# Products of probabilities with v issued for two key tiles in every second unit of attention

## The chip, the cores and the metric

The kernel runs on one core of one Trainium2 chip. The metric is device microseconds for one execution, and less is better. The core's engines each work through their own instructions in order and wait for each other by semaphores: TensorE (PE in the profile, its weight loads apart as PEld), VectorE (DVE), ScalarE (ACT), GpSimd (POOL), and SyncE (SP), which here issues most of the DMA.

## What is computed

Three layers one after the other, of which the change touches the first. Attention runs over 2 batches, 8 heads, 768 positions and a head dimension of 64; a query sees only the keys whose six projection signs equal its own. The layers behind it, a mixture of eight experts and a SoLU network, are not touched.

```python
q_bits = (np.einsum('bhsd,dk->bhsk', q, proj) > 0).astype(np.int64)
k_bits = (np.einsum('bhsd,dk->bhsk', k, proj) > 0).astype(np.int64)
mask = q_bucket[:, :, :, None] == k_bucket[:, :, None, :]
scores = scale * np.matmul(q, k.transpose(0, 1, 3, 2))
scores = np.where(mask, scores, -1000000000.0)
scores = scores - np.max(scores, axis=-1, keepdims=True)
attn = np.exp(scores)
attn = attn / (np.sum(attn, axis=-1, keepdims=True) + 1e-09)
return np.matmul(attn, v).astype(np.float32)
```

## The kernel before

**Units.** Attention is cut into 96 units. A unit is one tile of 128 queries of one head against all 768 keys. Six units (two heads by three query tiles) make a block j, and there are sixteen blocks; two blocks make one pair of heads n. The main loop (in the function that builds the kernel, behind the line that gets `emit_pv`) runs over the units i from 0 to 95 and records each unit's work; the order on every engine is the order in which the code records it, since the schedule is written by hand.

**What a unit i records**, in this order:

- `emit_s(i)` (L537): four matmuls of the scores s into one of two PSUM tiles, namely two halves of the keys, each first with the values and then with the sign bits. Between them and behind them stand the six transposes of the probabilities of unit i-2 (`steps_t`, L576), three into PSUM tile t0 and three into t1, with one buffer each. ScalarE copies each of the two to SBUF as pt (L578).
- in every sixth unit `fin_a` (L622): VectorE copies the finished sums v of a block from PSUM to xt. v has one PSUM buffer.
- `emit_max(i)` (L547, L549, L551): VectorE takes the largest score of each row, and two short steps behind it.
- `emit_exp(i)` (L562): ScalarE makes the probabilities p from s and the maximum.
- `emit_pv(jj, c)` (L595): the probabilities of block jj times v for the key tile c. For i from 8 to 91 jj and c are the quotient and the rest of i-8 by 6, so one of the six key tiles is done in each unit. It is two float32 matmuls, one for each head, which fill two halves of the columns; the trace shows each of them as two records. A block's tile c = 0 begins the sums in v, and c = 5 ends them.
- the background steps set for this unit. Those that matter here: `fin_b` in units 6j+14 (matmuls L638 from xt, on VectorE L627 to L658); `bits`, matmuls (L499 for q, L501 and L503 for k) and VectorE steps (L509) that make the sign bits of the next pair of heads, in units 5, 6, 9, 10 and 11 of each twelve; and, in three stretches, the routing of the next layer (`route_a` and others, L688 to L745).

So the order on PE within a unit is: scores and transposes, then the two v matmuls, then background matmuls. On ACT it is: the two copies of the transposes, then the exponential. On DVE: xt if there is one, the maximum, then background steps.

**What waits for what.** The scores of unit i need the PSUM tile that the exponential of unit i-2 has read. The transposes in unit i need the probabilities of unit i-2, and they need t0 and t1 to have been copied out by ACT, whose copies of the unit before stand behind the exponential of unit i-2. The v matmuls of c = 0 need the v tile to have been copied to xt; the L638 matmuls need xt itself.

**After the loop** the last blocks are done in other groupings (units 92 and 93 do three key tiles of block 14 each), and then come the experts.

Of the kernel before, what the change touches and what calls it, by code (L numbers as in the profile page):

```python
# [21 lines left out]
def kernel(  # L22
# [191 lines left out]
    def setup_first():  # L214


        fi = const.tile([128, 3], F32, name="fi")
        io = const.tile([128, 1], I32, name="io")
        nc.gpsimd.iota(io, pattern=[[0, 1]], base=0, channel_multiplier=1)
        nc.gpsimd.memset(pw, 0.0)  # L220
        d = nc.vector
        d.tensor_scalar(out=io, in0=io, scalar1=31, scalar2=None, op0=ALU.bitwise_and)
        d.tensor_copy(out=fi[:, 0:1], in_=io)
        d.tensor_scalar(out=fi[:, 1:2], in0=fi[:, 0:1], scalar1=float(NBIT), scalar2=-TINY, op0=ALU.is_ge, op1=ALU.mult)
        d.tensor_scalar(out=fi[:, 2:3], in0=fi[:, 0:1], scalar1=float(2 * NBIT), scalar2=TINY, op0=ALU.is_ge,
                        op1=ALU.mult)
        d.tensor_copy(out=thr[:, 1:2], in_=fi[:, 1:2])
        d.scalar_tensor_tensor(out=thr[:, 0:1], in0=fi[:, 1:2], scalar=TINY, in1=fi[:, 2:3], op0=ALU.add, op1=ALU.add)

    def setup_late():  # L230
        ie = const.tile([128, E], I32, name="ie")
        it = const.tile([128, B, NS], I32, name="it")
        g = nc.gpsimd
        g.memset(rb, 0.0)
        for h in range(2):
            r = slice(64 * h, 64 * h + 64)
            for wi, w in enumerate((w_gate, w_ogate)):
                c0 = 128 + 16 * h + 8 * wi
                nc.sync.dma_start(out=rb[r, :, c0:c0 + 8],
                                  in_=w.rearrange("(c h p) e -> h p c e", h=2, p=64)[h])  # L240
        nc.sync.dma_start(out=g1, in_=g_ln.rearrange("(f p) -> p f", p=128))
        g.iota(ie, pattern=[[1, E]], base=0, channel_multiplier=0)
        g.iota(it, pattern=[[S, B], [1, NS]], base=0, channel_multiplier=NS)
        make_upper_triangular(nc, upper, val=1.0, diag=False)
        g.memset(ones16, 1.0)
        g.memset(nhalf, -0.5)
        g.tensor_copy(out=iota8, in_=ie)
        g.tensor_copy(out=me[:, :, 1], in_=it.rearrange("p b s -> p (b s)"))
        g.tensor_scalar(out=iota_s, in0=iota8, scalar1=1.0 / 16.0, scalar2=1.0, op0=ALU.mult, op1=ALU.mult)
        g.tensor_scalar(out=ord0, in0=iota8, scalar1=-1.0, scalar2=1.0, op0=ALU.mult, op1=ALU.mult)  # L250
        for e in range(2):
            g.memset(ord0[:, e:e + 1], float(16 * NT * (2 - e)))
        for e in range(E):
            g.memset(caps[:, e:e + 1], float(CAPS[e]))
        for x in range(MW):
            g.memset(win_w[:, x:x + 1], float(WIN * x))
        g.tensor_scalar(out=row0, in0=iota8, scalar1=float(NT), scalar2=1.0, op0=ALU.mult, op1=ALU.mult)

        g.memset(hs, 0.0)
        g.tensor_scalar(out=hs[:, 0], in0=iota8, scalar1=float(NT // 128), scalar2=1.0, op0=ALU.mult, op1=ALU.mult)  # L260
# [617 lines left out]
    with tc.manual_schedule():  # L878
        with ExitStack() as es:
            A = attention(es)  # L880
            pj = A["pj"]
            cm, rb = A["cm"], A["rb"]
            setup_first()
            A["first"]()
            A["load"](1)
            setup_late()
            NU = A["NU"]
            bg = A["bg"]
            JL = 2 * NP - 2
            a_ = A.__getitem__  # L890
            pv, fa, tr = a_("emit_pv"), a_("fin_a"), a_("emit_t")
            for i in range(NU):
                a_("emit_s")(i, a_("steps_t")(i - 2) if 2 <= i else iter(()))
                if i in A["pre"]:
                    fa(A["pre"][i])
                a_("emit_max")(i)
                a_("emit_exp")(i)
                jj, c = divmod(i - 8, 6)
                if 0 <= jj < JL:
                    pv(jj, c)  # L900
                elif jj == JL and c < 2:
                    for x in range(3):
                        pv(JL, 3 * c + x)
                if i == NU - 3:
                    fa(JL, 0, 3, True)
                    a_("fin_r")(JL)
                if i == NU - 2:
                    a_("fin_mm")(JL)
                    a_("fin_l")(JL)
                    a_("fin_x")(JL)  # L910
                for f, a in bg.pop(i, []):
                    f(*a)
            assert not bg, bg.keys()

            J = JL + 1
            a_("route_a")(2)
            tr(NU - 2)
            for c in range(3):
                pv(J, c, 0, 2)
            a_("route_mm")(2)  # L920
            a_("route_b")(2)
            for c in range(3, NS):
                pv(J, c, 0, 2)
            fa(J, 0, 2)
            a_("fin_r")(J, 0, 2)
            a_("route_s")(2)
            tr(NU - 1)
            a_("fin_mm")(J, 0, 2)
            a_("fin_r")(J, 2, 3)
            for c in range(NS):  # L930
                pv(J, c, 2, 3)
            a_("fin_l")(J, 0, 2)
            a_("fin_x")(J, 0, 2, True)
            a_("route_a")(3)
            a_("route_mm")(3, tail=True)
            fa(J, 2, 3)
            a_("route_b")(3)
            a_("fin_mm")(J, 2, 3)
            a_("fin_l")(J, 2, 3)
            a_("route_a")(4)  # L940
            a_("route_mm")(4, (9, 10), True)
            a_("fin_x")(J, 2, 3, True, True)
            a_("route_b")(4)
            a_("route_s")(3)
            a_("totals")()
            for x in range(3):
                a_("route_d")(x, 2, 3, 4)
# [351 lines left out]
```

## Time and profile before

| | |
|---|---|
| median of 3 runs | 562.22 us (561.19 to 564.54) |
| time of the profiled execution | 566.43 us |
| its span, first to last instruction | 563.4 us |
| mean granted TensorE clock | 0.972 |
| PE busy | 515.2 us (91%), 3848 matmul records |
| DVE busy | 415.1 us (74%) |
| ACT busy | 339.6 us (60%) |
| POOL busy | 257.1 us (46%) |
| attention's units 8 to 91 | 28.23 to 242.91 us of the span |

The profile page gives busy times over the whole span, a strip of forty slices, the chain that ended last, and the costliest groups of instructions. The trace answers for single stretches: in a timeline each row has its start, its length, the engine, the line, the operation, output and inputs, and in brackets how long the engine sat idle before it and which instruction released it. Neighbouring records of one kind are merged into one row with their count.

### The profile page before, as it was taken

What the parts mean: (1) busy time and instruction counts of PE and PEld (TensorE: products, weight loads), DVE (VectorE), ACT (ScalarE), POOL (GpSimd) and SP (SyncE); (2) the same over time, 40 slices, a digit from 0 to 9 for tenths busy, and PEclk for the clock granted to TensorE, in tenths of its full rate; (3) what the DMA queues carried; (4) which work ended last, traced back from release to release, by engine and by line L of the source; (5) the groups of instructions that cost most, each with busy time, mean ns of one, the idle gap of its engine ahead of it and who ended that gap; (6) DMA issues with size and microseconds to landing.
All of it is one profiled execution on the core that took longest, in us unless ns stands there. A gap on an engine that the chain in (4) does not pass through costs nothing. (4 is left out here: it accounts for less than half of the span.)

```text
span 563.4 us, 10637 instructions
## 1 busy us (share of the span) xinstructions
PE 515.2 (91%) x3848; PEld 347.2 (62%) x3848; DVE 415.1 (74%) x929; ACT 339.6 (60%) x638; POOL 257.1 (46%) x321
## 2 busy tenths in 40 slices
PE   6799999999899999996499889599999999999994
PEld 5456565656555656664399789599997444444441
DVE  7877878788887898767339997799994776455440
ACT  6677787777667776863147866677572544344240
POOL 7968583838596674616036565222330111111112
PEclk9999999999999999999699999799999999999998
DMA  5576658554719263002498999999830242422542
GB/s 169 111 225 126 229 93 264 99 159 73 242 36 214 66 136 102 2 1 93 89 279 263 239 268 280 268 314 294 288 101 1 39 93 57 105 64 58 112 79 70
DMA packets 104487, 81.72 MB, mean 145 GB/s; under 512 B 79728, under 2 KB 86768, under 8 KB 104432
## 3 DMA queue, kind: packets, MB, share of 16 engines
q1 hardware_dynamic: 102128, 74.71, 51.5%
q0 software_dynamic: 2304, 6.31, 3.1%
q8 instruction: 31, 0.51, 0.4%
q14 instruction: 24, 0.20, 0.1%
HBM read 51.43 MB, written 9.97 MB: 109 GB/s over the span
## 5 line engine op out<-in xcount | busy, mean ns | idle before, releaser
L562 ACT ACTIVATE p<-s,mx 128x768 f32<-128x768 f32 x96 | 95.3, 992 | 55.4 <-DVE mx L551 46.0
L576 PE MATMUL t<-ident,p 128*128 128x128 f32 x576 | 126.1, 276 | 0.9 <-ACT pt L578 0.7
L547 DVE TENSOR_REDUCE mx<-s 128x1 f32<-128x768 f32 x96 | 91.7, 955 | 25.8 <-PE s L537 23.2
L578 ACT COPY pt<-t 128x384 f32<-128x384 f32 x192 | 84.7, 479 | 12.0 <-PE t L576 10.9
L576 PEld LDWEIGHTS t<-ident,p 128*128 128x128 f32 x576 | 78.4, 142 | 16.2 <-ACT pt L578 7.0
L1034 PE MATMUL a<-xw,wa 128*128 128x224 f16 (+5 forms) x256 | 65.4, 258 | 22.1 <-DVE yT L1075 12.1
L595 PE MATMUL v<-pt,v 128*64 128x384 f32 (+1 forms) x384 | 80.1, 503 | 2.9 <-DVE xt L622 2.5
L1045 POOL TENSOR_TENSOR hh<-hf,hh 128x448 f16<-128x448 f32 (+5 forms) x32 | 41.9, 1308 | 86.4 <-ACT hf L1044 86.3
L1246 PE MATMUL o<-wo,zT 128*128 128x512 f16 x288 | 64.0, 379 | 2.3 <-DMA zT<-z 2.3
L1035 PE MATMUL a<-xw,wa 128*128 128x224 f16 (+5 forms) x256 | 65.5, 258 | 0.0
L1036 PE MATMUL a<-xw,wa 128*128 128x224 f16 (+5 forms) x256 | 65.4, 258 | 0.0
L1065 PE MATMUL a<-hh,wb 128*128 128x224 f16 (+5 forms) x256 | 63.8, 252 | 0.5 <-DVE yT L1075 0.5
L1181 PE MATMUL h<-wi,yT 128*128 128x512 f16 x288 | 63.8, 379 | 0.1
L1066 PE MATMUL a<-hh,wb 128*128 128x224 f16 (+5 forms) x256 | 63.8, 252 | 0.0
L1067 PE MATMUL a<-hh,wb 128*128 128x224 f16 (+5 forms) x256 | 63.8, 252 | 0.0
L537 PE MATMUL s<-k,q 128*128 128x384 f16 x192 | 59.1, 332 | 4.0 <-ACT p L562 4.0
L537 PE MATMUL s<-b,cm 128*128 128x384 f16 x192 | 57.7, 328 | 1.1 <-DVE b L509 1.1
L1246 PEld LDWEIGHTS <-zT 128*128 128x128 f16 x288 | 27.9, 98 | 37.0 <-DMA zT<-z 3.7
L1181 PEld LDWEIGHTS <-yT 128*128 128x128 f16 x288 | 28.1, 98 | 34.1 <-DVE so L1207 0.6
L537 PEld LDWEIGHTS <-q 128*128 128x128 f16 x192 | 19.5, 102 | 39.6 <-issue 37.7
L1196 ACT ACTIVATE ex<-h,st,csc 128x1024 f32<-128x1024 f32 x12 | 14.5, 1204 | 44.3 <-DVE st L1219 36.0
L665 POOL TENSOR_SCALAR xh<-xf 128x384 f16<-128x384 f32 x15 | 7.7, 513 | 67.8 <-DVE xf L658 67.7
(241 smaller groups left out, 999.2 us busy)
## 6 DMA issues: line engine op xcount, KB each, us to landing
raw<-in_moe_w_dram SPq DMA_DIRECT2D x64, 512.0 KB, 5.3
raww<-in_moe_w_in_dram SPq DMA_DIRECT2D x8, 512.0 KB, 8.1
raww<-in_moe_w_out_dram SPq DMA_DIRECT2D x8, 512.0 KB
xs<-raw SPq DMA_DIRECT2D x8, 448.0 KB
v<-in_v_dram SPq DMA_DIRECT2D x8, 384.0 KB
q<-in_q_dram SPq DMA_DIRECT2D x7, 384.0 KB, 5.2
k<-in_k_dram SPq DMA_DIRECT2D x7, 384.0 KB, 4.5
cm<-q SPq DMA_DIRECT2D x14, 96.0 KB, 2.0
```

The costliest lines, as they stand in the source:

```text
L537: nc.tensor.matmul(t[:, c, 0:SB], d[x, h][:, s], flat(d[y, h])[:, c * SB:(c + 1) * SB], start=first, stop=not first)
L547: nc.vector.tensor_reduce(out=mx[:, 0:1], in_=t[:, :, 0:SB], op=ALU.max, axis=AX.XY)
L562: nc.scalar.activation(out=p, in_=s_t.pop(i)[:, :, 0:SB], func=AF.Exp, scale=mx[:, 1:2], bias=mx[:, 2:3], accum_out=sums[j][:, qt, h:h + 1])
L576: nc.tensor.transpose(t[:, g * 128:(g + 1) * 128], p[:, c, g * 128:(g + 1) * 128], ident)
L578: nc.scalar.copy(out=pt[j, h][:, 3 * c:3 * c + 3, qt * 128:(qt + 1) * 128], in_=t[:, 0:SB].rearrange("p (g c) -> p g c", g=3))
L595: nc.tensor.matmul(pv[j, q0][64 * h:64 * h + 64, 0:w], vt[:, h, c], pt[j, h][:, c, q0 * 128:q1 * 128], start=(c == 0), stop=(c == NS - 1), ...
L1034: nc.tensor.matmul(ps[:, i, 0:n], w[:, 0, kk, fs], xw[:, kk], start=(kk == 0), stop=False)
L1035: nc.tensor.matmul(ps[:, i, 0:n], w[:, 0, kk, fs], xw[:, KD + kk], start=False, stop=False)
L1036: nc.tensor.matmul(ps[:, i, 0:n], w[:, 1, kk, fs], xw[:, kk], start=False, stop=(kk == KD - 1))
L1065: nc.tensor.matmul(ps, w[:, 0, f, ds], hh[:, 0, f], start=(f == 0), stop=False)
L1181: nc.tensor.matmul(ps[:, c], yT[:, a, kk, ts], w_i[:, w, kk, c * 512:(c + 1) * 512], start=(kk == 0 and a == 0 and w == 0), stop=(kk == KD ...
L1246: nc.tensor.matmul(ps, zT[:, KF * a + f], w_o[:, w, f], start=(f == 0 and a == 0 and w == 0), stop=(f == KF - 1 and a == 1))
```

## The change

In units 8 to 91 the v matmuls are left out where the key tile c is even, and where c is odd those of c-1 and of c are recorded, in this order, at that place. As i-8 is even for even c, the even units record no v matmuls and the odd ones four. Unit 92 and those behind it are as before.

```diff
@@ -896,7 +896,8 @@
                 a_("emit_max")(i)
                 a_("emit_exp")(i)
                 jj, c = divmod(i - 8, 6)
-                if 0 <= jj < JL:
+                if 0 <= jj < JL and c % 2:
+                    pv(jj, c - 1)
                     pv(jj, c)
                 elif jj == JL and c < 2:
                     for x in range(3):
```

On PE, between units 24 and 25 (t are the transposes, v the products with the probabilities pt, s the scores of the next unit). Before:

```order
L576 MATMUL t_1107<-ident,p 128x128 x3
L595 MATMUL v<-pt_763,v 64x384
L595 MATMUL v<-pt_867,v 64x384
L537 LDWEIGHTS q_790
L537 MATMUL s<-k_853,q_790 128x384
L576 MATMUL t_1132<-ident,p 128x128
```

And now:

```order
L576 MATMUL t_1107<-ident,p 128x128 x3
L537 LDWEIGHTS q_787
L537 MATMUL s<-k_851,q_787 128x384
L576 MATMUL t_1130<-ident,p 128x128
L537 LDWEIGHTS q_787
```

The scores and transposes of unit 25 follow directly on the transposes recorded in unit 24.

On PE, at the end of unit 25. Before:

```order
L576 MATMUL t_1140<-ident,p 128x128 x3
L595 MATMUL v<-pt_763,v 64x384
L595 MATMUL v<-pt_867,v 64x384
L537 LDWEIGHTS q_790
L537 MATMUL s<-k_853,q_790 128x384
```

And now:

```order
L576 MATMUL t_1138<-ident,p 128x128 x3
L595 MATMUL v<-pt_763,v 64x384
L595 MATMUL v<-pt_865,v 64x384
L595 MATMUL v<-pt_763,v 64x384
L595 MATMUL v<-pt_865,v 64x384
L537 LDWEIGHTS q_787
```

Four v matmuls, for the key tiles 4 and 5 of the block, stand where two stood.

On PE, at the end of unit 26, where `fin_b` puts its matmuls m from xt. Before:

```order
L576 MATMUL t_1171<-ident,p 128x128 x3
L595 MATMUL v<-pt_964,v 64x384
L595 MATMUL v<-pt_1072,v 64x384
L638 MATMUL m<-rb,xt 128x160 x3
L537 LDWEIGHTS q_792
```

And now:

```order
L576 MATMUL t_1171<-ident,p 128x128 x3
L638 MATMUL m<-rb,xt 128x160 x3
L537 LDWEIGHTS q_789
L537 MATMUL s<-k_853,q_789 128x384
L576 MATMUL t_1205<-ident,p 128x128
```

The first matmuls that need VectorE's copy of the finished block are now those of L638. On the other engines the instructions stand in the order of before.

## Rows read from the trace of the kernel before

**Rows 1.** Busy time by engine in one cycle of twelve units; stretch, length, engines, PEclk, DMA share, GB/s
```profile
64.12:94.14 30.02, 29.90 (x208) 18.06 (x205) 24.13 (x56) 22.76 (x49) 19.41 (x22) 1.00 0.65 162
```
**Rows 2.** Waits in that cycle: engine, line, releaser; total, times, longest
```profile
ACT p L562 <- DVE mx L551: 7.2, 11, 0.9
```
**Rows 3.** PE timeline, first scores of units 6 and 7; unit 6 has no v matmuls
```profile
24.23 0.34 PE L537 MATMUL s<-k,q 128*128 128x384 f16 x1
...
25.55 0.33 PE L537 MATMUL s<-k,q 128*128 128x384 f16 x1
```
**Rows 4.** PE timeline, unit 93, which does three key tiles, and what follows in 94
```profile
247.32 0.33 PE L537 MATMUL s<-k,q 128*128 128x384 f16 x1
...
248.72 2.16 PE L595 MATMUL v<-pt,v 128*64 128x384 f32 x12
250.81 0.34 PE L537 MATMUL s<-k,q 128*128 128x384 f16 x1
...
252.13 0.98 PE L638 MATMUL m<-rb,xt 128*128 128x160 f32 x6
```
**Rows 5.** PE timeline, units 21 to 30 of that cycle
```profile
63.41 0.51 PE L501 MATMUL m<-k,pw 128*32 128x384 f16 x8
...
71.09 0.33 PE L576 MATMUL t<-ident,p 128*128 128x128 f32 x1
...
73.18 0.34 PE L537 MATMUL s<-k,q 128*128 128x384 f16 x1
...
75.38 1.08 PE L638 MATMUL m<-rb,xt 128*128 128x160 f32 x6
76.30 0.33 PE L537 MATMUL s<-k,q 128*128 128x384 f16 x1
76.46 0.27 PE L576 MATMUL t<-ident,p 128*128 128x128 f32 x1
...
78.50 0.34 PE L537 MATMUL s<-k,q 128*128 128x384 f16 x1
...
83.51 0.34 PE L537 MATMUL s<-k,q 128*128 128x384 f16 x1
```
**Rows 6.** PEld: the v matmuls' weight loads in that cycle; busy us, mean ns
```profile
L595 PEld LDWEIGHTS v<-pt,v 128*64 128x64 f32 x48 | 2.4, 134 | 2.2 <-issue 1.8 <-DVE xt L622 0.3
```
**Rows 7.** DVE timeline, units 22 to 27 of that cycle
```profile
66.81 1.25 DVE L509 TENSOR_SCALAR b<-m,thr 32x384 f16<-32x384 f32 x2
68.09 0.96 DVE L547 TENSOR_REDUCE mx<-s 128x1 f32<-128x768 f32 x1
...
69.52 0.62 DVE L509 TENSOR_SCALAR b<-m,thr 32x384 f16<-32x384 f32 x1
70.17 0.96 DVE L547 TENSOR_REDUCE mx<-s 128x1 f32<-128x768 f32 x1
...
72.23 0.96 DVE L547 TENSOR_REDUCE mx<-s 128x1 f32<-128x768 f32 x1 [0.66 <-PE s L537]
...
73.54 0.55 DVE L622 COPY xt<-v 128x384 f32<-128x384 f32 x1
...
75.75 0.22 DVE L627 TENSOR_SCALAR r<-sums 128x6 f32<-128x6 f32 x1
...
76.50 0.26 DVE L647 TENSOR_TENSOR lt<-m,r 128x96 f32<-128x96 f32 x1 [0.31 <-PE m L638]
...
77.56 0.95 DVE L547 TENSOR_REDUCE mx<-s 128x1 f32<-128x768 f32 x1
```
**Rows 8.** ACT timeline, exponential of unit 23
```profile
69.58 0.99 ACT L562 ACTIVATE p<-s,mx 128x768 f32<-128x768 f32 x1 [0.88 <-DVE mx L551]
```
**Rows 9.** PE timeline, unit 56, where routing work stands ahead of xt
```profile
151.27 0.87 PE L595 MATMUL v<-pt,v 128*64 128x384 f32 x4 [1.72 <-DVE xt L622]
```
**Rows 10.** Busy time by engine early in attention, and behind the wait of unit 56
```profile
15.00:28.00 13.00, 9.12 (x68) 6.08 (x65) 10.67 (x23) 8.65 (x18) 12.18 (x36) 1.00 0.59 120
...
152.50:155.90 3.40, 3.40 (x15) 2.64 (x13) 1.56 (x7) 1.56 (x3) 0.91 (x2) 0.50 0.03 10
```

## The prediction

> **What bounds the kernel now.** I first asked the trace for the busy time of one cycle of twelve units, the period after which the background work repeats. TensorE is busy 29.90 of 30.02 us at full clock (1.00, the 2.4 GHz level), VectorE 24.13 and ScalarE 22.76 [rows 1]. Read alone, that says that TensorE's work sets the end, and that any saving of it is a gain. So I asked next who waits for whom: nearly every exponential on ScalarE waits for VectorE's maximum (11 times, 7.2 us) [rows 2]. TensorE is full, but it runs just ahead of a chain that goes round every two units: last scores, maximum, exponential, then the transposes of these probabilities two units later. Third came the timelines of single units, to see how much slack that chain has, because the change alters the distance between a unit's scores and its transposes.
>
> **What is saved on TensorE.** A unit without v matmuls takes 25.55 - 24.23 = 1.32 us [rows 3], a plain one 78.50 - 76.30 = 2.20 [rows 5], so the two v matmuls of one key tile cost 0.89. Unit 93 does three key tiles and takes 250.81 - 247.32 = 3.49 [rows 4]: the second and third cost (3.49 - 2.20) / 2 = 0.645 each. Two key tiles together thus cost 1.54 where they cost 1.78, a saving of 0.245. The price is of the very form that the change makes, so I take it as it is.
>
> The Trainium skill speaks against so low a price: its page "TensorE: Matmul & The Clock Gate", section "Packing small matmuls — row/col tiling", says that a weight load overlaps running matmuls only if it goes to other rows of the array, and both v matmuls use all 128. By that rule a load, 0.134 us in the trace [rows 6], would stand ahead of each further tile and the saving would be about 0.11; the trace doesn't bear the rule out here, since the 0.645 of unit 93 already holds all loads.
>
> A second saving: the L638 matmuls now follow transposes, not v matmuls. Behind v they last 1.08 and the next scores come 0.92 after their start [rows 5], behind transposes they last 0.98 [rows 4]; I take 0.10 less, hence 0.82. A cycle has six merged pairs and two such places: 6 x 0.245 + 2 x 0.10 = 1.67 us. Units 8 to 91 are seven cycles: 11.7 us of TensorE's work.
>
> **What is added: waits.** The order of instructions on the other engines is unchanged, no DMA is moved, and POOL and SP get nothing new. What changes is that even units are short (1.32) and odd ones long (1.32 + 1.54 = 2.86). An odd unit's scores now come only 1.32 after the even unit's, not 2.20, and directly ahead of its transposes stand no v matmuls. The rule of the chain: the exponential starts 1.49 after its maximum (69.58 against 68.09) [rows 7, 8], and the first transposes that use it 1.51 after it (71.09 against 69.58) [rows 5, 8], ScalarE's copy of the unit before included. The maximum comes 1.26 after the unit's first scores (77.56 against 76.30) [rows 5, 7] if VectorE is free. From the transposes of one odd unit to those of the next that makes 1.26 - 0.16 + 1.49 + 1.51 = 4.10 of the 4.18 which a pair of units has now; of 4.41 before. So in plain pairs the new order just fits; wherever VectorE has extra work between the two maxima, TensorE must wait, and behind the waiting transposes stand in order the rest of the scores and all four v matmuls, whose operands are ready. That is the edit's real cost: a v pair that filled the wait in the even unit now comes after it.
>
> I walk through one cycle, with time 0 at unit 22 (64.12, where rows 1 begin).
>
> Units 22 to 25. Sign bits on VectorE hold it: the maximum of unit 23 comes at 68.09 - 64.12 = 3.97 and that of 24 at 6.05 [rows 7]. Both follow VectorE's own work without a gap and so stay. Before, unit 25 began at 6.6, three plain units on. Its transposes, which otherwise go 0.16 behind a unit's first scores (76.46 against 76.30) [rows 5], were held from 6.8 to 6.97 (71.09) by the exponential of unit 23. Now unit 25 could begin at about 5.5, but its transposes still go at 6.97: over a microsecond idle where 0.2 was. From there to the next unit it took 73.18 - 71.09 = 2.09 with one v pair [rows 5], 1.20 without; with two pairs unit 26 begins at 6.97 + 1.20 + 1.54 = 9.71, before at 9.06. **0.65 behind.**
>
> Units 26 and 27. L638 follows at once: 9.71 + 1.32 + 0.82 = 11.85, then 1.31 + 1.54, so unit 28 begins at 14.70, before at 14.38. 0.32 behind. But the maximum of unit 26 comes at 10.97; the next step on VectorE stands 1.31 behind a maximum (73.54 against 72.23), and from L627 to the maximum of unit 27 it is 77.56 - 75.75 = 1.81, of which 0.31 was waiting for L638 [rows 7]. So the maximum of 27 comes at 10.97 + 1.31 + 1.50 = 13.78, before at 13.44.
>
> Units 28 and 29. The exponential of 27 starts at 15.27, so the transposes of 29 go at 16.78, where TensorE would be ready at 14.70 + 1.32 + 0.16 = 16.18. A wait of 0.6: 16.78 + 1.20 + 1.54 = 19.52. With the bits matmuls (83.51 - 78.50 less two units of 2.20, 0.61) [rows 5] unit 30 begins at 20.13, before at 19.39. **0.74 behind.**
>
> Units 30 to 33. Two sign steps of 1.25 stand ahead of the maximum of 30 and two ahead of that of 31. Ahead of a maximum they cost 68.09 - 66.81 = 1.28, and the step behind one comes 69.52 - 68.09 = 1.43 later [rows 7]: maximum of 30 at about 21.5, of 31 at 24.2, xt from 25.5 to 26.1. TensorE, at unit 32 from 24.4, is done with its transposes at 25.7 and waits 0.4 for xt ahead of L638, then 0.82: unit 33 at 27.0. It ends 0.1 + 1.31 + 1.54 and the bits of k (64.12 - 63.41 = 0.71) [rows 5] later, at 30.66. Before: 30.02.
>
> **The sum.** A cycle gets 0.65 longer: 1.67 saved, and 2.3 more of waits than before. Seven cycles: 4.6 us. The profiled execution (span 563.4, time 566.43) would become 571.0. It lies 4.2 above the median of the runs; the cycles that I sum are regular ones, so I add the same to the median: 562.22 + 4.6 = 566.8. The bounds of a cycle are -1.67 (no new wait) and +2.3 (nothing of the saving counts, as VectorE and ScalarE set each pair): -11.7 and +16. I take the walk's value, since the rows on which its waits stand (71.09, 69.58, 68.09) belong to a wait of the same kind.
>
> In three stretches the routing adds VectorE work; in unit 56 v waited 1.72 us for xt [rows 9]. Now L638 waits there for the same copy. I count it as unchanged.
>
> **Rivals.** (A) TensorE's work sets the end after all: the chain's waits hide in slack that I count wrongly, and the saving comes through: 562.2 - 11.7 = 550.5, or half, 556. For it: 29.90 of 30.02 busy. Against it: the wait at 71.09 already exists with one v pair in the way. It decides if the transposes of unit 25 start well ahead of 6.97. (B) About even: the loss in units 24 and 25 is real, but the wait of 0.6 in unit 29 is not, because VectorE's steps behind L638 finish earlier now that L638 comes 0.33 sooner. Then a cycle is 0.0 to 0.2 longer, 562.2 to 563.7. It decides at the maximum of unit 27. (C) The clock falls more often. Behind the 1.72 of unit 56 TensorE ran 3.40 us at 0.50, the 1.2 GHz level [rows 10], which costs half of that, 1.70. Early in attention it was busy only 9.12 of 13.00 us and kept 1.00 [rows 10], and the new cycle is denser than that (some 27.9 of 30.7), so I give it little. Twice more makes 570.2, once in each cycle 578.7.
>
> **Chances.** The walk (564.5 to 571) 0.60; (B) with small gains or losses, 559.5 to 564.5, 0.20; (A) 0.12; (C), over 571, 0.08. The walk comes first because it gives the old cycle's starts to 0.1 us with the same numbers. 0.5% is about what a measurement of this kernel can tell from no change, 559.4 to 565.0. Part of the walk's low end lies in there, so: slower 0.65, same 0.23, faster 0.12. For 8 in 10 the range leaves out (A) and most of the far half of (C): 559.5 to 574.
>
> **What the profile after would show.** Right: unit 25's scores begin early and its transposes wait for ScalarE at about 7.0 after unit 22; TensorE's waits for p and pt, 0.2 us in unit 25 here, grow to over 1 us a cycle; L638 takes over the wait for xt; the four v matmuls and their gaps last about 1.54; a cycle takes 30.5 to 30.9. Wrong: cycles near 28.3 (A), a plain unit 29 without a wait (B), more stretches at 0.50 in attention (C), or v matmuls that cost 1.78 a pair of tiles.

## The result, and the profile after

The changed kernel takes 566.98 us (median of 16 runs) where the kernel before took 564.31 in the same comparison: a ratio of 1.0061, 95% interval 1.0045 to 1.0077, or 3.4 us of some 564 (2.5 to 4.3); the two medians alone differ by 2.67. It is slower, and by a little more than the 0.5% named ahead of it; forecast were 4.6 us, a ratio of 1.0082, just outside the interval. One of the 16 runs took 2592.68 us and has no part in the ratio. The profiled execution took 568.81 us with a span of 566.9 (before 566.43 and 563.4).

The first view is the page of the changed kernel: busy times, then groups (busy time, mean ns of one | idle time ahead of them, and what ended most of it). Under it are the same three groups before.

```profile
PE 509.4 (90%) x3848; PEld 349.4 (62%) x3848; DVE 417.1 (74%) x929; ACT 338.4 (60%) x638; POOL 260.0 (46%) x321
...
L576 PEld LDWEIGHTS t<-ident,p 128*128 128x128 f32 x576 | 77.7, 141 | 34.1 <-ACT pt L578 25.4
...
L595 PE MATMUL v<-pt,v 128*64 128x384 f32 (+1 forms) x384 | 70.8, 492 | 0.0
L537 PE MATMUL s<-k,q 128*128 128x384 f16 x192 | 59.6, 328 | 12.4 <-ACT p L562 12.3
```

```profile
L576 PEld LDWEIGHTS t<-ident,p 128*128 128x128 f32 x576 | 78.4, 142 | 16.2 <-ACT pt L578 7.0
...
L595 PE MATMUL v<-pt,v 128*64 128x384 f32 (+1 forms) x384 | 80.1, 503 | 2.9 <-DVE xt L622 2.5
...
L537 PE MATMUL s<-k,q 128*128 128x384 f16 x192 | 59.1, 332 | 4.0 <-ACT p L562 4.0
```

The v matmuls' busy time fell from 80.1 to 70.8 us for the same 384 instructions, and nothing waits ahead of them any more. What they gave back stands as idle time ahead of the scores (12.4 us, before 4.0) and of the transposes' loads (34.1, before 16.2), most of it ended by ScalarE.

The second view is the windows of one regular cycle (units 22 to 33), of the cycle with the routing (units 46 to 57) and of units 8 to 91, with the columns of [rows 1]; under it the two waits of the cycle that grew.

```profile
65.80:96.57 30.77, 29.24 (x209) 18.37 (x205) 24.25 (x56) 22.33 (x49) 19.30 (x23) 1.00 0.64 160
127.48:159.69 32.21, 29.32 (x212) 18.63 (x209) 26.83 (x70) 22.50 (x49) 23.21 (x28) 1.00 0.53 138
28.26:246.08 217.82, 204.36 (x1418) 127.88 (x1418) 175.49 (x428) 157.90 (x342) 140.84 (x159) 1.00 0.51 134
```

```profile
ACT p L562 <- DVE mx L551: 8.2, 11, 1.1
...
PEld t L576 <- ACT pt L578: 3.0, 5, 1.4
...
PE s L537 <- ACT p L562: 1.2, 2, 0.8
```

The cycle takes 30.77 us; it took 30.02 [rows 1], and the forecast was 30.66. TensorE is busy only 0.66 us less in it, as part of a wait still counts as busy: the transposes of unit 29 go 0.37 us behind its scores in place of 0.17, and the scores' matmul covers all but 0.05 of that. Its loads for the transposes wait for ScalarE's copies in five places, 3.0 us, and its scores for an exponential in two, 1.2 us. The surprise is in the second line. Before, these are the units around the wait of [rows 9], and they took 33.41 us:

```profile
124.16:157.57 33.41, 31.68 (x213) 19.24 (x209) 27.01 (x70) 23.08 (x49) 24.31 (x30) 0.95 0.50 133
28.23:242.91 214.68, 210.75 (x1418) 126.56 (x1418) 174.98 (x426) 159.54 (x342) 140.82 (x159) 0.99 0.52 136
```

So in these two executions the change gains 1.20 us there, and it loses everywhere else. But 1.70 of the 33.41 us are the stretch at half clock behind the wait (3.40 us at 0.50), and what is on record of the other executions speaks for most of them being without it, as the experiments will show. How far the changed kernel lies behind, by the starts of its scores in the two traces, and the same for a pair of kernels that comes up below:

| start of unit | 22 | 34 | 46 | 58 | 70 | 82 | 92 |
|---|---|---|---|---|---|---|---|
| changed less before, us | 1.68 | 2.43 | 3.32 | 2.12 | 2.22 | 2.55 | 3.17 |
| g2 less g1, us | 1.68 | 2.40 | 3.24 | 4.00 | 3.63 | 3.95 | 4.57 |

From unit 58 on, the first row holds these 1.70 us; without them the changed kernel would lie 4.87 behind at unit 92.

The third view is TensorE's timeline of the regular cycle (start, duration, and in brackets the idle time before and what ended it); subtract 65.80 to compare with the walk.

```profile
72.40 0.32 PE L537 MATMUL s<-k,q 128*128 128x384 f16 x1 [0.83 <-ACT p L562]
...
72.77 0.33 PE L576 MATMUL t<-ident,p 128*128 128x128 f32 x1
...
74.06 1.51 PE L595 MATMUL v<-pt,v 128*64 128x384 f32 x8
75.50 0.34 PE L537 MATMUL s<-k,q 128*128 128x384 f16 x1
...
76.82 0.98 PE L638 MATMUL m<-rb,xt 128*128 128x160 f32 x6
77.64 0.33 PE L537 MATMUL s<-k,q 128*128 128x384 f16 x1
...
80.48 0.34 PE L537 MATMUL s<-k,q 128*128 128x384 f16 x1
...
82.33 0.32 PE L537 MATMUL s<-k,q 128*128 128x384 f16 x1 [0.37 <-ACT p L562]
82.70 0.33 PE L576 MATMUL t<-ident,p 128*128 128x128 f32 x1
...
86.03 0.34 PE L537 MATMUL s<-k,q 128*128 128x384 f16 x1
...
92.04 1.08 PE L638 MATMUL m<-rb,xt 128*128 128x160 f32 x6 [0.23 <-DVE xt L622]
92.96 0.33 PE L537 MATMUL s<-k,q 128*128 128x384 f16 x1
...
96.57 0.34 PE L537 MATMUL s<-k,q 128*128 128x384 f16 x1
```

In order: unit 25's first scores and transposes, its two key tiles' v products in one row, unit 26, its L638, units 27 and 28, the first scores and transposes of 29, unit 30, L638 of unit 32, units 33 and 34. On VectorE the maxima of units 26 and 27 stand so, with L627 between them:

```profile
76.76 0.96 DVE L547 TENSOR_REDUCE mx<-s 128x1 f32<-128x768 f32 x1 [0.59 <-PE s L537]
...
78.08 0.25 DVE L627 TENSOR_SCALAR r<-sums 128x6 f32<-128x6 f32 x1
...
79.72 0.94 DVE L547 TENSOR_REDUCE mx<-s 128x1 f32<-128x768 f32 x1
```

### The profile page after: what moved, and what is told of

The parts are those of the page before. It is cut to its first block, busy times and chain, and to the rows that moved or that the text cites. A ratio compares the mean times of both kernels' runs of the same rounds, so it can differ in the third digit from the quotient of the medians.

```text
span 566.9 us, 10632 instructions
## 1 busy us (share of the span) xinstructions
PE 509.4 (90%) x3848; PEld 349.4 (62%) x3848; DVE 417.1 (74%) x929; ACT 338.4 (60%) x638; POOL 260.0 (46%) x321
## 5 line engine op out<-in xcount | busy, mean ns | idle before, releaser
L576 PEld LDWEIGHTS t<-ident,p 128*128 128x128 f32 x576 | 77.7, 141 | 34.1 <-ACT pt L578 25.4
L595 PE MATMUL v<-pt,v 128*64 128x384 f32 (+1 forms) x384 | 70.8, 492 | 0.0
L537 PE MATMUL s<-k,q 128*128 128x384 f16 x192 | 59.6, 328 | 12.4 <-ACT p L562 12.3
L595 PEld LDWEIGHTS v<-pt,v 128*64 128x64 f32 x384 | 23.5, 136 | 24.5 <-issue 23.8
```

What stands on the lines that cost most here:

```text
L537: nc.tensor.matmul(t[:, c, 0:SB], d[x, h][:, s], flat(d[y, h])[:, c * SB:(c + 1) * SB], start=first, stop=not first)
L576: nc.tensor.transpose(t[:, g * 128:(g + 1) * 128], p[:, c, g * 128:(g + 1) * 128], ident)
L595: nc.tensor.matmul(pv[j, q0][64 * h:64 * h + 64, 0:w], vt[:, h, c], pt[j, h][:, c, q0 * 128:q1 * 128], start=(c == 0), stop=(c == NS - 1), ...
```

## The experiments

My theory was the one on record: saved TensorE time turns into waits on the chain of maximum, exponential and transposes, at three places (unit 25, unit 29, L638 of unit 32). The main rival was that doing two key tiles in a row costs by itself. The kernel before took 561.72 us beside e1, e2, e3 and e5, 561.21 beside f1 to f4, and 561.29 beside g1 to g3.

### The pairs in the even units

```diff
-                if 0 <= jj < JL and c % 2:
-                    pv(jj, c - 1)
+                if 0 <= jj < JL and c % 2 == 0:
                     pv(jj, c)
+                    pv(jj, c + 1)
```

> The two key tiles are joined in the even units instead: unit 6j+8+c, c even, does c and c+1. Theory (place): TensorE's work is the same as in the changed kernel, but the four v matmuls stand between an even unit's transposes and the odd unit's scores, where the exponentials of the odd units are waited for. Walked as in the prediction, with time 0 at unit 22: unit 24 at 4.2, unit 25 at 7.0 with its transposes ready at 7.19 and allowed from 7.1, so no wait; unit 26 at 8.3, waits to about 9.2 for the exponential of unit 24; unit 28 at 14.15, 30 at 18.9, 32 at 23.1, then 0.4 of wait for xt; a cycle of 29.45 where before takes 30.02. Seven cycles: 4.0 us faster than before, ratio 0.993. Rival (joining): four v matmuls in a row cost what they cost wherever they stand, since two units' products come at once and the other engines starve meanwhile: as the changed kernel, ratio 1.006.

Measured: 564.45 us, ratio 1.0046 (1.0029 to 1.0063). The number missed, and the interval holds the 1.006 of the rival; what decides against that rival are e2, f2 and f3 below. The wait of unit 25 is gone as the theory had it, unit 28 begins 14.14 us after unit 22 (changed kernel 14.68), and yet the cycle takes 30.15:

```profile
63.60:93.75 30.15, 29.38 (x208) 18.46 (x205) 24.06 (x57) 22.52 (x48) 19.25 (x23) 1.00 0.70 173
```

On VectorE, around the maxima of units 29 to 31:

```profile
81.97 0.96 DVE L547 TENSOR_REDUCE mx<-s 128x1 f32<-128x768 f32 x1 [1.10 <-PE s L537]
...
83.40 1.23 DVE L509 TENSOR_SCALAR cm<-m,thr 32x384 f16<-32x384 f32 x2
84.66 0.96 DVE L547 TENSOR_REDUCE mx<-s 128x1 f32<-128x768 f32 x1
...
86.09 1.25 DVE L509 TENSOR_SCALAR cm<-m,thr 32x384 f16<-32x384 f32 x2
```

The two sign steps behind the maximum of unit 29 put that of unit 30 at 1.94 us after its scores in place of 1.26, and the next pair that of 31 at 1.79. I had counted these steps for the joined odd units and forgotten them here. The wait only moved to another unit; and unit 56 cost more here too, a wait of 2.21 us for xt and, from 0.16 us before its end, 3.4 us at 0.50.

### Sign steps of k out of the way, in the changed kernel and in the one before

```diff
-                ((9, "k"), (0,)), ((10, "k"), (1, 2)), ((11, "k"), (3,)))
+                ((9, "k"), (0, 1)), ((11, "k"), (2, 3)))
```

> The changed kernel with VectorE's sign steps of k moved: tiles 0 and 1 in unit 9 of each twelve, 2 and 3 in unit 11, so that none stands between the maximum of unit 22 and that of unit 23. Theory (VectorE's steps between the two maxima make the wait): maximum of 23 at 2.9 instead of 3.97, its exponential at 4.4, transposes of unit 25 at 5.9 instead of 6.97, unit 26 at 8.6 instead of 9.7, a cycle of about 29.55 against 30.77 in the changed kernel and 30.02 before: 3 us faster than before, ratio 0.994. Rival (joining costs by itself): unit 26 still at 9.7, cycle 30.7, ratio 1.006.

> The kernel before with the same move of the sign steps of k, as the control of the run with the changed kernel. Theory: only the 0.17 us (0.23 with what follows) of wait in unit 25 goes, a cycle of 29.8, 1.6 us in all: ratio 0.997. Rival (the move by itself is what helps): as much as with the changed kernel, ratio 0.99 or less.

Measured: the changed kernel with the move 560.5 us, 0.9979 (0.9960 to 0.9998); the kernel before with it 561.69, 0.9992 (0.9970 to 1.0014), no difference. In the changed kernel the maximum of unit 23 comes 1.46 us after its scores (2.66 without the move), unit 25's transposes go at 6.19 after unit 22 in place of 6.97, and unit 26 starts 0.78 sooner. It comes through to the end of the cycle:

```profile
64.71:94.79 30.08, 29.29 (x209) 18.37 (x205) 24.26 (x56) 22.19 (x49) 19.46 (x23) 1.00 0.75 199
```

So the same four VectorE steps, done a little elsewhere, are worth 0.7 us a cycle to the joined order and nothing to the other: this part of the loss is VectorE's work between two maxima, and joining doesn't cost by itself. It gave less than forecast because with the maximum sooner the exponential of unit 23 waited 1.89 us behind it, not 1.49: between two exponentials ScalarE has two copies of pt to do.

### Units 24 and 25 with single tiles

```diff
-                if 0 <= jj < JL and c % 2:
+                if 0 <= jj < JL and i % 12 in (0, 1):
+                    pv(jj, c)
+                elif 0 <= jj < JL and c % 2:
```

> The changed kernel, but in units 0 and 1 of each twelve (24 and 25 of the shown cycle) one key tile each as before; the five other pairs are joined. Theory: the pair in units 24 and 25 alone makes the loss. Unit 26 at 9.06 as before, unit 28 at about 14.05, 30 at 19.5, 33 at 26.8, a cycle of 30.0 to 30.1: ratio 1.000. Rival (joining costs by itself, the same in each pair): five sixths of the loss stay, ratio 1.005.

Measured: 562.45 us, 1.0012 (0.9994 to 1.0031), which holds the theory's 1.000 and not the rival's 1.005. In the cycle shown, unit 26 begins at 9.06 after unit 22 as forecast, unit 28 at 14.03, but unit 30 at 20.21 where 19.5 was forecast, and the cycle takes 30.75. What went wrong stands in two rows, one of VectorE and one of GpSimd:

```profile
76.79 0.88 DVE L627 TENSOR_SCALAR r<-sums 128x6 f32<-128x6 f32 x1
```

```profile
75.85 1.79 POOL L339 TENSOR_TENSOR kl<-k,ks 128x384 f16<-128x384 f32 x2
```

A step on six elements a partition lasted 0.88 us in place of 0.25, and it ended (77.67) as GpSimd's instruction ended (77.64). Time won ahead of it put it under that instruction, and the maximum of unit 27 came no sooner. In the next cycle the step falls where one of these GpSimd instructions follows on the other, and takes 0.16 us; the units that answer to 26, 28 and 30 begin 9.06, 14.04 and 19.50 us after its start, and the cycle is as forecast:

```profile
95.91:125.93 30.02, 29.39 (x208) 18.31 (x205) 24.07 (x56) 22.33 (x49) 19.39 (x23) 1.00 0.52 134
```

### The same, with the held step a unit sooner

```diff
+        def fin_r0(j):
+            r_t[j] = sm.tile([128, 3, 2], F32, tag="r", name="r", bufs=2)
+            fin_r(j)
...
-            fin_r(j)
...
+            at(6 * j + 13, fin_r0, j)
```

> The kernel with the pair of units 24 and 25 left apart, and VectorE's two steps on r (L627 and L629 there) done one unit sooner, in unit 6j+13. In the run without this move the first of them lasted 0.88 us instead of 0.16 to 0.25 and ended as GpSimd's L339 ended. Theory (the step on r is held while GpSimd runs L339, and that gives the gain of the pair left apart back in units 28 and 29): lt can start as soon as the maximum of unit 26 is done, the maximum of unit 27 comes at about 12.8 after unit 22 instead of 13.9, unit 30 begins at about 19.2 instead of 20.2, a cycle of about 29.75; ratio 0.997. Rival (something else holds unit 29, the step on r only fills the wait): unit 30 still at 20.2, cycle 30.7, ratio 1.001.

Measured: the cycle does what was forecast, the time doesn't: 29.73 us from unit 22 to unit 34, but 563.36 us in all, 1.0033 (1.0007 to 1.0060). In the regular cycle the step takes 0.16 us, the maximum of unit 27 comes at 12.67 after unit 22 and unit 30 at 18.99, which confirms the hold by GpSimd. In unit 56 the same step fell under another GpSimd instruction, now ahead of xt:

```profile
149.31 1.75 DVE L633 TENSOR_SCALAR r<-sums 128x6 f32<-128x6 f32 x1
```

```profile
152.05 1.08 PE L644 MATMUL m<-rb,xt 128*128 128x160 f32 x6 [2.37 <-DVE xt L622]
```

```profile
153.30:156.70 3.40, 3.40 (x15) 1.88 (x15) 2.27 (x6) 2.37 (x5) 2.09 (x3) 0.50 0.01 2
```

L638 (L644 there) waited 2.37 us, and behind it TensorE ran 3.40 us at 0.50, the 1.2 GHz level: units 46 to 57 took 33.26 us.

### Even pairs with the waits taken out one by one

```diff
-        BITS = (((5, "q"), (0, 1)), ((6, "q"), (2, 3)),
-                ((9, "k"), (0,)), ((10, "k"), (1, 2)), ((11, "k"), (3,)))
+        BITS = (((5, "q"), (0,)), ((6, "q"), (1, 2)), ((7, "q"), (3,)),
+                ((9, "k"), (0, 1)), ((10, "k"), (2, 3)))
...
-            pre[6 * j + 14] = j
+            pre[6 * j + 13] = j
```

f2 joins in even units, copies xt a unit sooner and moves the k steps; f3 (the diff, on top of the even pairs) moves those of q as well; f4 is the kernel before with f3's order of sign steps alone. There xt can't be copied sooner, since a block's last v products stand in unit 6j+13 itself.

> Joined in the even units, xt copied one unit sooner (the sums are complete at the end of unit 6j+12 there), and the sign steps of k in units 9 and 10, two each, so that none stands between the maxima of units 23 and 24. Theory (place and VectorE's steps): the wait of unit 26 shrinks from 0.66 to 0.15, that for xt in unit 32 goes, a cycle of 29.0 to 29.2 against 30.16 with the joined even units alone and 30.02 before: 6 us faster than before, ratio 0.99. Rival (joining costs by itself): ratio 1.004, as with the even units alone.

> As the kernel before this one, and the sign steps of q as one, two, one in units 5, 6 and 7, so that one step and not two stands ahead of the maximum of unit 30. Theory: the maximum of unit 30 comes 0.6 sooner, the wait of unit 32 (0.6 with what follows) goes, a cycle of about 28.6: 9 to 10 us faster than before, ratio 0.983. Rival (VectorE's steps don't set this wait): as the kernel before this one, 0.99.

> The kernel before with the same order of the sign steps of k and q, nothing joined: the control. Theory: TensorE's work sets nearly all of the cycle before, and only its waits of 0.2 to 0.4 a cycle can go: 29.7 to 30.0, ratio 0.996 to 1.000. Rival (the gain comes from the order of VectorE's steps and not from joining): as the kernel joined in the even units.

Measured: f2 558.68 us, 0.9951 (0.9934 to 0.9967); f3 557.4, 0.9924 (0.9898 to 0.9949); f4 564.98, 1.0058 (1.0037 to 1.0079). The cycles of f3 and f4:

```profile
63.25:92.74 29.49, 29.25 (x209) 18.46 (x205) 24.25 (x57) 22.32 (x48) 19.35 (x23) 1.00 0.71 176
```

```profile
65.15:96.17 31.02, 30.12 (x208) 18.08 (x205) 24.86 (x56) 22.70 (x49) 19.37 (x22) 1.00 0.68 161
```

The joined pairs, with steps that suit them, beat both kernels. The same steps without them are slower than before, where f4 was forecast to be no slower: a sign step of q now stands ahead of xt in unit 32, and v waits for it.

```profile
91.55 0.87 PE L595 MATMUL v<-pt,v 128*64 128x384 f32 x4 [0.75 <-DVE xt L622]
```

So joining in even units, with the sooner xt that it allows, is worth 7.6 us (564.98 - 557.4) under f3's order of steps, of which 3.3 are what that order costs the kernel before (f4); against the kernel before itself f3 gains 4.3 us. Under the old order the same even pairs cost 2.6 us (e1). What the sooner xt gives by itself no run tells. The cycles came out longer than forecast, though (f2 29.92 against 29.0 to 29.2, f3 29.49 against 28.6): in f2 q's steps still put the maximum of unit 31 at 2.26 us after its scores, and in both a unit with an exponential close behind another still waits in front of its transposes (0.37 in place of 0.17 us behind its scores, in units 24 and 26).

### Is unit 56 the step that was off?

The routing's two small VectorE steps (L744, L745) stand ahead of xt there. L745 adds 128x8 numbers. In the changed kernel, with GpSimd's row:

```profile
153.47 1.22 DVE L745 TENSOR_TENSOR hs<-hs,hn 128x8 f16<-128x8 f16 x1
```

```profile
152.55 2.13 POOL L183 TENSOR_TENSOR wa<-raw,wa 128x1024 f16<-128x1024 f32 x1
```

Here too the small step ends (154.69) with GpSimd's (154.68). Two kernels, before and changed, and f3 as a third, got these two steps two units later:

```diff
-        for x, f, g in ((3, route_a, 0), (4, route_mm, 0), (4, route_b, 0), (7, route_s, 0),
+        for x, f, g in ((3, route_a, 0), (4, route_mm, 0), (4, route_b, 0), (9, route_s, 0),
```

> The kernel before with the routing's two small VectorE steps (L744, L745) put two units later, behind unit 57 in place of unit 55, so that they no longer stand ahead of the copy xt of unit 56. My theory: the change loses 3.4 us and not the 4.6 forecast because unit 56, which I had counted as unchanged, costs the kernel before more than the changed one: there TensorE waited 1.72 us for xt and then ran 3.4 us of time at half clock. If so, xt starts about 1.4 us sooner here, the wait shrinks to about 0.3, the stretch at half clock is gone (1.7 us of work in place of 3.4), units 46 to 58 take about 30.3 us in place of 33.41 and units 8 to 92 about 211.6 in place of 214.7: ratio to the kernel before 0.9945. Rival (the fall of the clock has nothing to do with that wait): only the 1.4 us of the wait go, the clock still falls somewhere, ratio 0.9975.

> The changed kernel with the same two steps moved in the same way. Theory: L638's wait in unit 56 goes from 1.58 to about 0.4, units 46 to 58 take 31.1 us in place of 32.21, units 8 to 92 about 216.7: ratio to the kernel before 1.004. Set against the kernel before with the same move, the change then costs 5 us, about 1.0095, which is the 4.6 us that the seven cycles were forecast to lose, and a little. Rival (unit 56 is not where the forecast was off): the distance of the two stays at 3.4 us, about 1.006.

> The order that beat both kernels (v products joined in even units, xt copied a unit sooner, the sign steps of k and q moved up), with the routing's two steps two units later as well. Its wait of 1.40 us for xf in unit 57 came from the same held step (1.32 us): it should shrink to about 0.2 and units 46 to 58 go from 31.05 to 29.9: ratio to the kernel before 0.990 where it was 0.9924. Rival: the two steps in their new place delay the row maximum of unit 58 and nothing is won, 0.992 to 0.993.

Measured: g1 559.61 us, 0.9958 (0.9938 to 0.9978); g2 564.07, 1.0049 (1.0029 to 1.0068); g3 555.61, 0.9905 (0.9876 to 0.9934). The windows of units 46 to 57, of g1 and of g2:

```profile
124.11:154.23 30.12, 30.00 (x212) 18.15 (x209) 25.30 (x68) 22.73 (x49) 23.19 (x29) 1.00 0.55 147
```

```profile
127.35:158.23 30.88, 29.37 (x212) 18.55 (x209) 25.47 (x68) 22.47 (x49) 23.19 (x29) 1.00 0.54 144
```

The held step and what follows from it are gone: L745, now in unit 57, takes 0.19 us in g1,

```profile
155.21 0.19 DVE L745 TENSOR_TENSOR hs<-hs,hn 128x8 f16<-128x8 f16 x1
```

v no longer waits for xt in unit 56, the clock keeps 1.00, and the 33.41 us of the kernel before become 30.12, a regular cycle (forecast 30.3). In g2 L638's wait goes from 1.58 to 0.23 us. Without this place the change costs 4.46 us (564.07 - 559.61); the quotient of the two ratios is 1.0091, and as each is uncertain by 0.002 it lies between about 1.006 and 1.012. The times leave the rival open, and g1's interval holds both of its forecasts. In the table above the two pairs lie equally far behind up to unit 46, and from there the pair with the place loses 1.20 less in one cycle and the pair without it 0.76 more. At unit 92 it is 4.57 us, of which 0.50 arose before unit 8, where both programs are the same.

That difference hangs on the half clock in the one profiled execution of the kernel before, and three other records speak against taking it as the rule. First, e3 is the kernel before with four sign steps moved. Its v waits as long for xt in unit 56, its clock stays at 1.00, and units 46 to 57 take 31.69 us:

```profile
151.13 0.87 PE L595 MATMUL v<-pt,v 128*64 128x384 f32 x4 [1.70 <-DVE xt L622]
```

```profile
124.06:155.75 31.69, 30.00 (x212) 18.15 (x209) 26.88 (x70) 22.70 (x49) 23.17 (x29) 1.00 0.53 140
```

f4 waits even longer there and keeps 1.00 too:

```profile
154.30 0.87 PE L595 MATMUL v<-pt,v 128*64 128x384 f32 x4 [1.82 <-DVE xt L622]
```

Second, every execution has its mean granted clock on record, profiled or not. It averages 0.9771 over 77 executions of the kernel before (those beside the experiments), 0.9774 over 99 of the ten kernels, the changed one among them, whose profile shows no half clock inside attention, and 0.9739 over 24 of e1 and f1, whose profiles show it. Such a stretch takes 1.70 / 563 = 0.003 off the mean. Third, units 8 to 91 of the kernel before take 214.68 us in its profile. Less 1.70 they make 212.98, and measured from there the profiled lengths of ten of the twelve other kernels lie within the intervals of their ratios; measured from 214.68, six do. So most executions of the kernel before, by my estimate, are without the stretch; with about 31.7 us for its units 46 to 57, the changed kernel's 32.21 are 0.5 longer.

g3 is the fastest kernel of this study; its gain over f3 (1.8 us by the medians) is inside their uncertainty. In the trace its units 46 to 57 take 29.61 us in place of 31.06, but units 58 to 69 take 31.27 in place of 30.36.

## Why the prediction was right, and where it was off

**TensorE's saving: right.** A unit with two key tiles takes 80.48 - 77.64 = 2.84 us and one with none 1.31 to 1.32, so the pair costs 1.53; the forecast was 1.54. L638 behind the transposes of unit 26 lasts 0.98 and the next scores come 0.82 after its start, as taken; in unit 32, where it waits for xt, it is 1.08 and 0.92 as before, so that this second saving comes once a cycle and not twice. By the Trainium skill's rule that was weighed (page "TensorE: Matmul & The Clock Gate", section "Packing small matmuls — row/col tiling") a pair would have cost 1.67, an estimate (1.78 less 0.11); the trace doesn't agree with it here.

**Units 22 to 25: right in time, wrong in the place of the wait.** Transposes of unit 25 at 72.77 - 65.80 = 6.97 and unit 26 at 9.70 (forecast 6.97 and 9.71). But unit 25's scores didn't begin early: they begin at 6.60, as before, and not at about 5.5, since TensorE stands idle 0.83 us ahead of them already. They wait for the exponential of unit 23, which has to read the scores in their PSUM tile first; the walk had only the transposes wait for it. As it is the same exponential, unit 26 began when forecast. Taking this wait away (e2) gave 0.69 us a cycle back, which shows it as a cause.

**Units 26 to 29: right within 0.15.** Maximum of unit 27 at 13.92 (13.78 forecast: VectorE's steps between the two maxima took 1.64 us, not 1.50), unit 28 at 14.68 (14.70), transposes of 29 at 16.90 (16.78), unit 30 at 20.23 (20.13). Here too the scores wait already (0.37 us). Rival (B) was decided against at this maximum, as the prediction said it would be. f1 shows how near it was: with units 24 and 25 left apart and L627 a unit sooner, unit 30 comes at 18.99.

**Units 30 to 33: right in kind.** L638 stands where v stood, waits for xt (0.23 us at its matmuls), unit 33 begins at 27.16 (27.0) and the cycle ends at 30.77 (30.66). New waits of a cycle: 30.77 - (30.02 - 1.67) = 2.42 us, and 2.3 with L638's saving counted once; forecast 2.3.

**The sum: near, in part because its errors cancel.** In the two profiles units 8 to 91 lose 3.14 us where the sum had 4.55. The largest error there is the sentence on unit 56, "I count it as unchanged". Before, a wait of 1.72 us for xt was followed by 3.40 us at half clock [rows 9, 10]; in the changed kernel the wait is 1.58 us,

```profile
155.22 1.08 PE L638 MATMUL m<-rb,xt 128*128 128x160 f32 x6 [1.58 <-DVE xt L622]
```

and TensorE keeps 1.00 behind it. The cycle came out 1.20 shorter, not 0.65 longer, 1.85 us off the sum. But 1.70 of that is the half clock, which by the estimate above most executions of the kernel before don't have. Without it the cycle is 0.5 longer, so that "unchanged" was near, and units 8 to 91 lose 4.84 us.

The other parts err both ways. The first fourteen units lost 1.65 us where 0.65 a cycle gives 0.76; 0.65 of it in unit 9, which begins at the same time as before, waits for the exponential of unit 7 and then does two key tiles; the rest I have not followed. The two cycles from unit 22 to 46 lost 1.64 where 1.30 was forecast. In the second place with routing work (units 58 to 69) the change lost 0.09, not 0.65: its matmul L709, which waited 0.65 us before for VectorE's oh_all, waits 0.30 now; in g1 and g2 it is 1.01 and 0.21. There the new waits of TensorE lie beside one that it had anyway. Units 70 to 91 lost 0.95 where 1.19 was forecast.

So the mechanism, the walk of a regular cycle and its sign stand; "seven times the same" was the weak part of the sum. That the predicted 566.8 us lies so near the measured 566.98 is partly luck, as the kernel before was 2.1 us slower in that comparison than in the runs shown with it; the difference is what tells, 3.4 against 4.6.

**What stays open.** Where the 1.4 us between the 4.84 of units 8 to 91 and the measured 3.4 come back is not shown. Behind unit 92, where the code is the same in all kernels, the profiled executions take 316.3 to 320.8 us, so one execution of each can't tell. g1 is 2.4 us faster by its ratio, with an interval of 1.2 to 3.5 us; the wait that is gone explains 1.6 of it (31.69 in e3 against 30.12), less 0.36 that units 58 to 69 lose again. What makes the clock fall in some executions and not in others with the same wait is open too.

## What to carry to other kernels

A kernel that looks bound by one full engine can still be paced by a chain through others; work saved on the full engine then counts only as far as the chain's next link is ready, and the order of small steps on the other engines decides the sign (here +3.4 us for the changed kernel and -1.2 for e2, which joins the same matmuls). When a sum is made over equal cycles, walk the cycles that are not equal by themselves. Before a cause is put on a stretch that one profiled execution shows, look whether a kernel with the same wait has it, and what clock the other executions were granted. And before moving a small step, look at what the neighbouring engine runs at that moment: in e5 and f1 here a tiny instruction was held by a long one.

## What the runs showed of the hardware

Two of VectorE's small steps were held until a running GpSimd instruction ended: L627 0.88 us (e5) and, in its new place, 1.75 us (f1) in place of 0.16 to 0.25, L745 1.48 us before and 1.22 after in place of 0.16 to 0.19. In g3 its new place put L745 beside another GpSimd instruction, and it took 1.03 us. Other steps were not held: L744, which stands just ahead of L745, took 0.17 us under the same instruction. The maxima, which read PSUM, took 0.93 to 0.96 us in all profiles, beside whatever GpSimd did. The Trainium skill has this (page "SBUF — State Buffer", section "Who interferes with whom"): VectorE and GpSimd share a pair of ports, and whichever instruction takes it first keeps it to its end. The ends of the held rows agree with that within 0.03 us.

In the profiled executions TensorE fell to 0.50 inside attention in three kernels, each time at unit 56's wait for xt or just behind it: 1.72 us (before), 2.21 (e1) and 2.37 (f1). It kept 1.00 there in all others, with waits of 1.58 us (changed kernel), 1.70 (e3) and 1.82 (f4) among them, so the length of the wait alone did not decide it. Where it fell, the wait cost its own length and half of the 3.40 us more.
